# A gated spectral mixer with its gradients on one core: the opening's first folds ordered behind the last scaling of the second token block

## The chip, the core and the metric

The kernel runs on one core of a Trainium2 chip. A core has five engines, each with its own instruction queue that runs strictly in the order in which it was written: TensorE (PE, matrix products, with its weight loads shown as PEld), VectorE (DVE), ScalarE (ACT), GpSimd (POOL) and SyncE (SP). SP here does nothing but issue DMAs; POOL and ACT issue some too. Engines wait for one another through semaphores. The metric is the device time of one execution in microseconds (us); several executions are timed and the median is given. Beside them one execution is recorded by the hardware profiler, and that record is what this document reads.

## The reference, cut to what matters

A forward pass of two branches, mixed by a gate that depends on the token, and then the gradient of everything:

```python
g = sigmoid((x * gate_w).sum(-1, keepdims=True))
a = irfft2(rfft2(x) * (w_r + 1j * w_i))              # spectral branch, over tokens and features
h = relu(x @ w1 + b1); b = (h * h) @ w2 + b2       # dense branch, of the same x
out = g * a + (1 - g) * b
grads = vjp(out)(grad_out)     # for x, w_r, w_i, w1, b1, w2, b2, gate_w
```

There are 2048 tokens of 1024 features, 3584 hidden units, and everything in memory is bf16. The gradient of the dense branch's output is `grad_out` scaled by `1 - g`, one factor per token; that of the spectral branch is `grad_out` scaled by `g`.

## The kernel before

**What the opening does.** Tokens are handled as 16 rows (tiles) of 128 tokens, four rows to a block. For each block four things have to happen before its products can run: the four rows of `x` are loaded into `xsrc` buffers and turned (transposed on TensorE against an identity into a PSUM tile `pt`, then copied to `xT`); the gate of the block is computed; the four rows of `grad_out`, loaded into `dbn`, are scaled in place by `omg` = 1 - g; and the scaled rows are turned the same way into `dbT`. `turn_x`, `turn_grad`, `gate_of` and `gate` do these. `gate_of` (L724) is one long DVE instruction for each row, `x * gate_w` with a running sum; `gate` (L731, L732, L734) is two tiny sigmoids on ACT over the four sums and then four DVE scalings. The two `pt` tiles are used in turn, so that a third transposition waits until the copy of the first is through.

**The products.** Chains of eight matmuls into one PSUM bank. `ph` (L808 in half widths, L821) is a hidden block: x by w1; ACT empties it with a ReLU (L822), and a square (L795) makes `h2T`. `pd` (L828) is the gradient at the hidden layer, `dbT` by the transposed w2; DVE empties it with one instruction (L832, `dhT`). In the opening `ph` and `pd` share two banks, so each chain also waits for the eviction of the one before the last.

**The first stage of the spectral branch.** `first_stage` runs in between, as a generator that the opening's loop advances now and then. It takes pairs of rows (`xs[0]`, `xs[1]`, ..., tiles named `src`, loaded by `ahead_to`, first on SP's queue). `folds` makes sums and differences of a pair on DVE: two into `uv` (L272, L273), then L277, L278, L283 and L284 into `f`, with tiny ACT copies between (L279, L281, L285). `row_stage` then multiplies on TensorE (`pk`, L293) and ACT copies the result to `ft` (L297). `first_columns` follows (`pu`, L325, emptied by three ACT instructions L303 to L307), then two more DVE instructions (L312, L313) and stores.

**What sets the order.** Nobody writes the queues by hand: a scheduler takes the program, its dependencies and priorities and emits each engine's queue. Its freedom is limited with ties. `after(ins, earlier, NoSync)` adds a dependency that orders `ins` behind `earlier` for the scheduler, and without a wait of its own on the chip where both are on the same engine; `after` without that argument also makes `ins` wait. The name `later["last"]` holds the newest eviction of a `pd` product (set in `back_`, L883), and `first_stage` ties its steps to it: the first two folds of each pair, the first matmul of `row_stage` and of `first_columns`, and, through `ahead_to`, the loads of the next pair. The first stage begins in the loop over blocks at k = 0, right behind the gate of the second block:

```python
if k + 1 < NT // 4:
    gate(4 * (k + 1))
if k + 2 < NT // 4:
    rows_of_x(k + 2)
if k == 0:
    ahead_to(1)
    stage = first_stage()
next(stage)
```

At that point the newest `pd` eviction is the second one of the first block (the one before the two that follow in the loop). `next(stage)` runs `folds` for pair 0, the first `row_stage`, and `ahead_to(2)`, which loads pair 2.

Of the kernel before, what the change touches and what calls it, by code (L numbers as in the profile page):

```python
# [14 lines left out]
ALU = mybir.AluOpType  # L15
# [126 lines left out]
def kernel(  # L142
# [22 lines left out]
    nc = tc.nc  # L165
# [43 lines left out]
    gcol, omg, gpg, dgs, dsc = (cols(n, [NT]) for n in ("gcol", "omg", "gpg", "dgs", "dsc"))  # L209
# [40 lines left out]
    def after(ins, earlier, wait=mybir.DependencyClass.Sync):  # L250

        if earlier is not None:
            info = mybir.DependencyInfo(wait, mybir.DependencyReason.DATA)
            tc.add_manual_dep(ins.ins, earlier.ins.name, info, reason="paced")
# [15 lines left out]
    def folds(fb, xt, earlier=None):  # L270
        uv = fb.tile([P, 2, 2, H], FDT, name="uv", tag="uv")
        after(V(out=uv[:, :, 0, :], in0=xt[:, :, 0:H], in1=xt[:, :, H:D], op=ALU.add), earlier, mybir.DependencyClass.NoSync)  # L272
        after(V(out=uv[:, :, 1, :], in0=xt[:, :, 0:H], in1=xt[:, :, H:D], op=ALU.subtract), earlier, mybir.DependencyClass.NoSync)  # L273

        f = fb.tile([P, 2, 6, Q + 2], FDT, name="f", tag="f", bufs=2)
        a0, a1 = uv[:, :, :, 1:Q], uv[:, :, :, H - 1 : Q : -1]
        V(out=f[:, :, 0:2, 1:Q], in0=a0, in1=a1, op=ALU.add)  # L277
        V(out=f[:, :, 2:4, 1:Q], in0=a0, in1=a1, op=ALU.subtract)  # L278
        nc.scalar.copy(out=f[:, :, 3:0:-2, 0], in_=uv[:, :, 1, 0 : Q + 1 : Q])  # L279

        nc.scalar.copy(out=f[:, :, 0:3:2, 0 : Q + 1 : Q], in_=uv[:, :, 0:1, 0 : Q + 1 : Q].to_broadcast([P, 2, 2, 2]))  # L281
        b0, b1 = f[:, :, 0:3:2, 0:P], f[:, :, 0:3:2, Q:P:-1]
        V(out=f[:, :, 4:6, 0:P], in0=b0, in1=b1, op=ALU.add)  # L283
        V(out=f[:, :, 4:6, P:Q], in0=b0, in1=b1, op=ALU.subtract)  # L284
        nc.scalar.copy(out=f[:, :, 5, P::-P], in_=f[:, :, 0:3:2, P])  # L285
        return f

    def row_stage(fb, f, kmat, earlier=None):
        pk = fps.tile([P, 8, P], FP32, name="pk", tag="ps2", bufs=2)
        even = [(row, slice(o, o + P)) for row, o in ((5, P), (4, 0), (4, P), (5, 0))]  # L290
        odd = [(row, slice(o, Q, 2)) for row, o in ((3, 0), (3, 1), (1, 1), (1, 0))]
        for b, (row, o) in enumerate(even + odd):
            first_ = mm(pk[:, b, :], lhsT=f[:, row, o], rhs=kmat[:, b // 6, :], start=True, stop=True)  # L293
            if b == 0:
                after(first_, earlier, mybir.DependencyClass.NoSync)
        ft = fb.tile([P, 8, P], FDT, name="ft", tag="ft", bufs=2)
        nc.scalar.copy(out=ft[:], in_=pk[:])  # L297
        return ft

    def first_columns(cf, t, ft, u, w, earlier=None):  # L300
        pu = fps.tile([P, 2, H], FP32, name="pu", tag="ps2", bufs=2)
        column_stage(pu, ft, cf, earlier)
        nc.scalar.copy(out=w[:, t].rearrange("p c x g i -> p (c x g i)"), in_=pu[:, 1, :])  # L303
        uv = u[:, t].rearrange("p (c h g i) -> p c h g i", c=2, h=2, g=4)
        even = pu[:, 0, :].rearrange("p (g c h i) -> p c h g i", g=2, c=2, h=2)
        nc.scalar.copy(out=uv[:, 0, :, 0::2, :], in_=even[:, 0])
        nc.scalar.mul(out=uv[:, 1, :, 0::2, :], in_=even[:, 1], mul=flip[:])  # L307

    def odd_columns(T, i, u, w):
        uv = u[:].rearrange("p t (c h g i) -> p (t c) h g i", c=2, h=2, g=4)  # L310
        X, Y = (w[:].rearrange("p t c x g i -> p (t c) x g i")[:, :, x] for x in range(2))
        V(out=uv[:, :, 0, 1::2, :], in0=X, in1=Y, op=ALU.add)  # L312
        V(out=uv[:, :, 1, 3::-2, ::-1], in0=X, in1=Y, op=ALU.subtract)  # L313
        nc.gpsimd.tensor_copy(out=edge[:, :, T, i : i + 2], in_=u[:, :, 0::H].rearrange("p t x -> p x t"))
        moved(z_scr, T, i, u, True)
# [377 lines left out]
    dbn = db_p.tile([P, NT, D], BF16, name="dbn", tag="dbn")  # L693
# [4 lines left out]
    later = {}  # L698
# [28 lines left out]
    def gate(i0):  # L727

        c_ = slice(i0, i0 + 4)
        pg = pgs[:, c_]  # L730
        nc.scalar.activation(omg[:, c_], pg, ACT.Sigmoid, scale=-1.0)  # L731
        nc.scalar.activation(gcol[:, c_], pg, ACT.Sigmoid)  # L732
        for i in range(i0, i0 + 4):
            nc.vector.tensor_scalar(out=dbn[:, i, :], in0=dbn[:, i, :], scalar1=omg[:, i : i + 1], scalar2=None, op0=ALU.mult)  # L734

    def ahead_to(n, earlier=None):
        for j in range(len(xs), min(n + 1, NT)):
            xs[j] = f1.tile([P, 2, D], BF16, name="src", tag="src", bufs=3)
            for t in range(2):
                T, i = divmod(2 * j + t, NT)  # L740
                after((ld if j < 3 else st)(out=xs[j][:, t, :], in_=(go_perm if T else x_perm)[i]), earlier)

    def first_stage():
        f, kg = {0: folds(f1, xs[0], later["last"])}, {}
        for j in range(NT):
            T, i = divmod(2 * j, NT)
            ft = {}
            for t in range(2):
                ft[t] = row_stage(f1, f[j][:, t], kg.pop(2 * j + t)[:] if T else kf[:], later["last"])
                if t == 0:  # L750
                    ahead_to(j + 2, later["last"])
                yield
                if t == 0 and j + 1 < NT:
                    for n in range(2 * j + 2, 2 * j + 4) if 2 * j + 2 >= NT else ():
                        kg[n] = f1.tile([P, 2, P], FDT, name="kg", tag="kg", bufs=3)
                        g_ = gcol[:, n - NT : n - NT + 1]
                        scaled = nc.vector.tensor_scalar(out=kg[n][:], in0=kf[:], scalar1=g_, scalar2=None, op0=ALU.mult)
                        after(scaled, later["last"], mybir.DependencyClass.NoSync)
                    f[j + 1] = folds(f1, xs[j + 1], later["last"])
            u = f1.tile([P, 2, D], FDT, name="u", tag="xsrc", bufs=3)  # L760
            w = f1.tile([P, 2, 2, 2, 2, P // 2], FDT, name="w", tag="w")
            for t in range(2):
                first_columns(cf, t, ft[t], u, w, later["last"])
                if t:
                    odd_columns(T, i, u, w)
                yield
        f1_s.close()
# [1051 lines left out]
    def rows_of_grad(k, n=4, lo=0):  # L1819
        for i in range(4 * k + lo, 4 * k + lo + n):  # L1820
            ld(out=dbn[:, i, :], in_=go_perm[i])
# [7 lines left out]
    def turn_grad(i):  # L1829
        turn_tile(dbT, i, dbn[:, i, :], nc.scalar.copy if i in (1, 3) else nc.vector.tensor_copy)  # L1830
# [36 lines left out]
    for k in range(NT // 4):  # L1867
        i = 4 * k
        if k + 1 < NT // 4:
            rows_of_grad(k + 1)  # L1870
        next(units)
        if k:
            turn_grad(i), turn_grad(i + 1)
        next(units)
        turn_grad(i + 2) if k else gate(0)
        next(units)
        if k:
            turn_grad(i + 3)
        else:
            for to, name in ((kf, "kf"), (flip, "flip"), (sel, "sel"), (cf, "cf")):  # L1880
                after(st(out=to[:], in_=cten[name].ap()), later["newest"])
            for n in range(4):
                turn_grad(n)
        next(units)
        if stage:
            next(stage)
        next(units)
        if k + 1 < NT // 4:
            turn_x(i + 4), turn_x(i + 5)
        next(units)  # L1890
        if k + 1 < NT // 4:
            turn_x(i + 6), turn_x(i + 7)
        next(units)
        for n in ((), (0,), (4, 8), (12,))[k]:
            after(st(out=db_scr[:, n : n + 4, :], in_=dbn[:, n : n + 4, :]), later["last"])
        if k + 1 < NT // 4:
            gate(4 * (k + 1))
        if k + 2 < NT // 4:
            rows_of_x(k + 2)
        if k == 0:  # L1900
            ahead_to(1)
            stage = first_stage()
        next(stage)
        if k == 3:
            for _ in later["x_sums"](0):
                pass
        next(units)
        next(stage)
# [45 lines left out]
    out = later["out"]  # L1954
# [36 lines left out]
```

## Time and profile before

| what | value |
|---|---|
| median of 3 executions | 1196.62 us (1193.79, 1196.62, 1200.95) |
| the profiled execution | 1195.43 us |
| its span, first to last instruction | 1193.6 us |
| mean granted clock of TensorE | 0.999 of full |
| PE busy | 1174.1 us |
| DVE, ACT, POOL busy | 895.3, 531.0, 388.6 us |

The profiled execution's own time is 1.83 us longer than its span. A line of a timeline gives the start in us from the beginning of the span, the duration (for several merged instructions: of the group), the engine, the line of the kernel, the operation, the tile written and the tiles read, the shape, and how many instructions were merged; in brackets stands how long the engine had been idle before and what ended that. Matmuls overlap, so the duration of one group reaches a little past the start of the next; the step from group to group is the time that counts. A few matmul records are missing from a trace, so that a chain of eight may show as seven.

### The profile page before, as it was taken

To read this page: it belongs to the slowest core of one execution; us is meant where nothing else is said; L and a number is where in the kernel's file an instruction comes from. 1 tells how busy PE (TensorE), PEld (TensorE's weight loads), DVE (VectorE), ACT (ScalarE), POOL (GpSimd) and SP (SyncE) were. 2 spreads that over 40 slices of the span, in tenths; PEclk is the share of its full clock that TensorE was granted. 3 is DMA by queue.
4 is the path that set the end of the run, shared out by engine and by line. 5 is a ranking of instruction groups with operands and counts; after the bars stand their busy time and mean duration, and the time that the engine had idled before them with its cause. 6 is when DMAs were issued, how large, how long until landed. Compare 5 with 4: busy or idle time off the path is not lost.

```text
span 1193.6 us, 19422 instructions
## 1 busy us (share of the span) xinstructions
PE 1174.1 (98%) x7198; PEld 643.2 (54%) x7291; DVE 895.3 (75%) x1598; ACT 531.0 (44%) x961; POOL 388.6 (33%) x618
## 2 busy tenths in 40 slices
PE   8899999999999999999999999999999999999998
PEld 6555555444444444444446999998544444444444
DVE  5888887688989787877537666666786677976757
ACT  5577888577777773445224565654200010000000
POOL 0224443565857683764231332221001100000000
PEclk9999999999999999999999999999999999999999
DMA  9898585676969879889996999995889999564530
GB/s 255 279 261 245 176 210 178 204 202 176 241 175 214 254 249 179 208 177 228 205 225 139 236 231 246 249 210 158 259 194 235 247 283 282 178 195 149 180 125 36
DMA packets 329464, 249.84 MB, mean 209 GB/s; under 512 B 187912, under 2 KB 287658, under 8 KB 328858
## 3 DMA queue, kind: packets, MB, share of 16 engines
q1 hardware_dynamic: 268352, 112.12, 44.7%
q0 software_dynamic: 35136, 111.72, 29.6%
q10 hardware_dynamic: 25882, 24.76, 7.2%
q8 instruction: 57, 0.93, 0.3%
q14 instruction: 37, 0.30, 0.1%
HBM read 114.82 MB, written 89.67 MB: 171 GB/s over the span
## 4 chain that ended last, share of the span: by engine, by line
PE 72%; DVE 15%; issue 4%; DMA 3%; ACT 3%; POOL 1%; SPq 1%; ACTq 0%; another core or an unknown queue 0%; DVEq 0%; POOLq 0%
PE pX L1277 15%; PE xX L1578 14%; PE pV L1277 11%; PE pd L828 8%; PE xV L1578 7%; PE ph L929 4%; PE xZ L1578 3%; PE ph L821 2%; DVE rT L948 2%; DVE dhT L832 1%; PE pui L325 1%; DVE tt L453 1%; PE pki L635 1%; PE pu L325 1%; PE pk L293 1%
## 5 line engine op out<-in xcount | busy, mean ns | idle before, releaser
L828 PE MATMUL pd<-dbT,w2T 128*128 128x512 bf16 x862 | 207.9, 380 | 3.7 <-DVE dhT L832 1.6
L828 PEld LDWEIGHTS <-w2T 128*128 128x128 bf16 x896 | 86.7, 98 | 106.0 <-issue 7.4
L1578 PEld LDWEIGHTS <-dS 128*128 128x128 f16 x686 | 66.4, 98 | 78.6 <-issue 3.0
L832 DVE SCALAR_TENSOR_TENSOR dhT<-pd,rT 128x512 bf16<-128x512 f32 x112 | 76.5, 683 | 33.4 <-PE pd L828 33.0
L1629 POOL DMA_DIRECT2D out_dram<-ot x32 | 17.4, 544 | 245.8 <-DVE ot L1685 128.0
L1695 ACT ACTIVATE w2br<-w2br,dsc 128x512 f32<-128x512 bf16 x8 | 5.8, 724 | 173.8 <-DVE ot L1685 117.4
L1578 PE MATMUL xX<-oT,dS 128*128 128x512 f16 x336 | 76.4, 379 | 0.2 <-DVE eR L1607 0.2
L1293 ACT COPY u<-pX 128x512 f32<-128x512 f32 x56 | 32.8, 586 | 90.5 <-PE pX L1277 84.9
L1578 PEld LDWEIGHTS <-odd 128*128 128x128 bf16 (+1 forms) x462 | 44.8, 98 | 51.5 <-issue 0.9
L1578 PEld LDWEIGHTS <-even 128*128 128x128 bf16 (+1 forms) x448 | 43.7, 98 | 52.6 <-issue 0.7
L1277 PEld LDWEIGHTS <-T 128*128 128x128 f16 x672 | 64.6, 98 | 7.4 <-issue 0.2
L949 ACT ACTIVATE rT<-rT 128x512 bf16<-128x512 bf16 x69 | 43.4, 629 | 44.2 <-DVE rT L948 43.7
L795 ACT ACTIVATE h2T<-rT 128x1024 bf16<-128x1024 bf16 x56 | 59.7, 1065 | 0.2
L1297 DVE TENSOR_TENSOR whi<-pV,u 128x512 bf16<-128x512 f32 x28 | 19.3, 688 | 47.2 <-ACT u L1293 47.1
L1277 PEld LDWEIGHTS <-S 128*128 128x128 f16 x336 | 32.5, 98 | 40.8 <-DVE S L1209 1.9
L491 POOL DMA_DIRECT2D y_scr<-pc x64 | 47.2, 738 | 18.6 <-DVE pc L488 11.3
L453 DVE TENSOR_TENSOR tt<-x,w 128x1028 f16<-128x1028 f16 (+1 forms) x64 | 43.9, 719 | 10.6 <-ACT x L445 4.6
L1277 PEld LDWEIGHTS <-resL 128*128 128x128 bf16 x448 | 43.1, 98 | 4.9
L1277 PEld LDWEIGHTS <-resR 128*128 128x128 f16 (+1 forms) x448 | 43.0, 98 | 4.9 <-issue 0.2
L860 POOL DMA_DIRECT2D h2T_scr<-h2T x28 | 20.9, 746 | 70.1 <-ACT h2T L795 43.3
L1297 DVE TENSOR_TENSOR wlo<-pV,u 128x512 bf16<-128x512 f32 x28 | 19.2, 687 | 32.0 <-PE pV L1277 31.9
L239 POOL DMA_DIRECT2D r<-y_scr x48 | 28.0, 588 | 41.7 <-ACT re L614 33.1
(382 smaller groups left out, 2797.9 us busy)
## 6 DMA issues: line engine op xcount, KB each, us to landing
h2T_scr<-h2T POOLq DMA_DIRECT2D x28, 512.0 KB, 4.4
dhT_scr<-dhT POOLq DMA_DIRECT2D x28, 512.0 KB, 5.3
y_scr<-pc POOLq DMA_DIRECT2D x64, 128.0 KB, 4.2
ax_scr<-yo POOLq DMA_DIRECT2D x16, 512.0 KB, 5.5
out_dram<-ot POOLq DMA_DIRECT2D x31, 256.0 KB, 3.9
z<-z_scr ACTq DMA_DIRECT2D x60, 128.0 KB, 3.8
out_dram<-whi POOLq DMA_DIRECT2D x28, 256.0 KB, 4.9
out_dram<-wlo POOLq DMA_DIRECT2D x28, 256.0 KB, 5.6
```

What stands on the lines that cost most here:

```text
L239: st(out=a, in_=b) if stored else st(out=b, in_=a)
L453: V(out=tt[:, k, :, :, 0:W], in0=x[:, a : a + 2, :, 0:W], in1=by, op=ALU.mult)
L491: st(out=columns_of(y_scr, c, h), in_=pc[:, n])
L795: after(nc.scalar.activation(h2T, rT, ACT.Square), behind_, mybir.DependencyClass.NoSync)
L828: turn["PE"] = mm(pd[:], lhsT=w_[:, ec, fc % FGC * P : (fc % FGC + 1) * P], rhs=dbT[:, ec, ss], start=(ec == 0), stop=(ec == DC - 1),)
L832: return STT(out=dhT, in0=pd[:], scalar=2.0, in1=rT, op0=ALU.mult, op1=ALU.mult, accum_out=gb1part[:, fc, sb : sb + 1],)
L929: turn["PE"] = mm(acc[:], lhsT=lhs[:, t, :], rhs=rhs[:, t, :], start=start and t == 0, stop=t == KH - 1, skip_group_check=True,)
L949: nc.scalar.activation(rT, rT, ACT.Relu)
L1277: self.mm = mm(out, lhsT=lhs[:, t, m * P : (m + 1) * P], rhs=rhs[:, t, :], start=start and t + a == 0, stop=t == KH - 1, skip_group_check= ...
L1293: turn["ACT"] = nc.scalar.copy(out=t_[:], in_=self.X[:])
L1297: turn["DVE"] = self.added = V(out=self.half(row, j), in0=self.sums(acc), in1=self.sums(t_), op=ALU.add)
L1578: ins = mm(acc, lhsT=lhs[:, fc, :], rhs=rhs[:, fc, :], start=start and fc == 0, stop=fc == KH - 1 and bias is None, skip_group_check=True,)
```

## The change

The last of the four scalings is handed out of `gate`, and the loop puts the one of the second block (rows 4 to 7, `gate(4)` at k = 0) into `later["last"]` just before it starts the first stage. The next `pd` eviction overwrites that again, as before.

```diff
@@ in gate
         for i in range(i0, i0 + 4):
-            nc.vector.tensor_scalar(out=dbn[:, i, :], in0=dbn[:, i, :], scalar1=omg[:, i : i + 1], scalar2=None, op0=ALU.mult)
+            scaled = nc.vector.tensor_scalar(out=dbn[:, i, :], in0=dbn[:, i, :], scalar1=omg[:, i : i + 1], scalar2=None, op0=ALU.mult)
+        return scaled
@@ in the loop over blocks
         if k + 1 < NT // 4:
-            gate(4 * (k + 1))
+            scaled = gate(4 * (k + 1))
         if k + 2 < NT // 4:
             rows_of_x(k + 2)
         if k == 0:
             ahead_to(1)
+            later["last"] = scaled
             stage = first_stage()
         next(stage)
```

So pair 0's two folds, the first `row_stage` and the loads of pair 2 are tied to that scaling. No instruction is added or removed. The queues around the place, before and after:

| queue | before | after |
|---|---|---|
| DVE | sums of rows 4, 5; dhT; sum of row 6; L272; sum of row 7; L273; 4 scalings; L277, L278; dhT; L283, L284; folds of pair 1; dbT copy; ... | sums of rows 4, 5; dhT; sums of rows 6, 7; 4 scalings; L272, L273; dhT; L277, L278; dbT copy; L283, L284; folds of pair 1; dbT copy; ... |
| ACT | ReLU; two sigmoids; ReLU; L279; square; ... | sigmoid; ReLU; sigmoid; ReLU; square; L279; ... |
| PE | pd; turn rows 4, 5; pd but one matmul; 16 pk; last of pd; 2 of ph; turn row 6; rest of ph; turn row 7; ... | pd; turn rows 4, 5; pd; turn row 6; 2 of ph; 16 pk; rest of ph; turn row 7; ... |
| SP | pair 1's second row; pair 2; 8 rows of grad_out; ... | pair 1's second row; 3 rows of grad_out; pair 2; 5 rows of grad_out; ... |
| POOL | | the same |

Some 20 us on, a few transposes, `pd` matmuls and the next block's folds stand one or two places apart from before; from about 60 us the queues are the same.

## The prediction

> **What bounds the kernel now.** I read the page first, then the granted clock in slices of one microsecond, then the timelines of PE, DVE, ACT and SP between 20 and 45 us. From the page, the shares of the engines:
>
> ```profile
> PE 1174.1 (98%) x7198; PEld 643.2 (54%) x7291; DVE 895.3 (75%) x1598; ACT 531.0 (44%) x961; POOL 388.6 (33%) x618
> ```
>
> PE is busy for 1174.1 of 1193.6 us, so all its idle time is 19.5 us, and an edit that adds and removes no work has little to win. The stretch from 30 us on holds its largest hole. By microseconds (window, length, PE busy and matmuls, granted clock, DMA share, GB/s):
>
> ```profile
> 30.00:31.00 1.00, 0.31 (x2) 1.00 1.06 391
> ...
> 33.00:34.00 1.00, 0.00 (x0) 0.86 1.06 385
> 34.00:35.00 1.00, 0.84 (x9) 0.50 1.04 383
> ...
> 36.00:37.00 1.00, 1.00 (x4) 0.50 1.06 393
> 37.00:38.00 1.00, 1.00 (x5) 0.94 1.06 391
> ```
>
> PE stops at 30.31, its clock falls to one half at about 33.86 (0.86 of that slice) and returns at about 37.06. The timeline of PE (start, length, line, operation, how many, idle before and what ended it):
>
> ```profile
> 24.83 3.69 PE L808 MATMUL ph<-xT,w1g 128*128 128x256 bf16 x32
> 28.42 1.89 PE L828 MATMUL pd<-dbT,w2T 128*128 128x512 bf16 x7
> 34.16 1.89 PE L709 MATMUL pt<-identb,dbn 128*128 128x128 bf16 x16 [3.85 <-DVE dbn L734]
> 35.84 2.32 PE L828 MATMUL pd<-dbT,w2T 128*128 128x512 bf16 x7
> 38.08 1.07 PE L293 MATMUL pk<-kf,f 128*128 128x128 f16 x16
> ...
> 39.20 0.59 PE L821 MATMUL ph<-xT,w1g 128*128 128x512 bf16 x2
> 39.64 0.61 PE L709 MATMUL pt<-identb,dbn 128*128 128x128 bf16 x8
> ...
> 42.31 1.89 PE L821 MATMUL ph<-xT,w1g 128*128 128x512 bf16 x8
> 44.04 0.40 PE L325 MATMUL pu<-cf,ft 128*128 128x128 f16 x4
> 44.27 1.89 PE L828 MATMUL pd<-dbT,w2T 128*128 128x512 bf16 x8
> ```
>
> The transposes of grad_out rows 4 and 5 wait 3.85 us for their scaling (L734). DVE tells why it is late:
>
> ```profile
> 25.60 1.22 DVE L724 SCALAR_TENSOR_TENSOR Sw<-xsrc,Sw 128x1024 bf16<-128x1024 bf16 x1
> ...
> 31.26 0.69 DVE L272 TENSOR_TENSOR uv<-src 128x1024 f16<-128x1024 bf16 x1 [4.43 <-DMA src<-in_A_x_dram]
> 31.87 1.22 DVE L724 SCALAR_TENSOR_TENSOR Sw<-xsrc,Sw 128x1024 bf16<-128x1024 bf16 x1
> 33.02 0.08 DVE L724 DVE_READ_ACCUMULATOR Sw<-xsrc,Sw 128x1 f32 x1
> 33.02 0.68 DVE L273 TENSOR_TENSOR uv<-src 128x1024 f16<-128x1024 bf16 x1
> 33.62 1.67 DVE L734 TENSOR_SCALAR dbn<-dbn,omg 128x1024 bf16<-128x1024 bf16 x4
> 35.20 0.68 DVE L277 TENSOR_TENSOR f<-uv 128x1020 f16<-128x1020 f16 x1
> ...
> 36.41 0.68 DVE L832 SCALAR_TENSOR_TENSOR dhT<-pd,rT 128x512 bf16<-128x512 f32 x1
> ...
> 37.36 0.42 DVE L284 TENSOR_TENSOR f<-f 128x512 f16<-128x512 f16 x1
> ```
>
> The first fold (L272) stands ahead of the fourth gate sum and idles DVE for 4.43 us until its source has landed; the sum, the gate and the scalings queue behind it. That load releases PE here.
>
> **The change, part by part.** It adds and removes no instruction. Compared engine by engine, the streams differ from about 27 to 60 us only and are the same afterwards; POOL's is the same throughout.
>
> *Fold behind scaling: the hole.* DVE's order becomes fourth sum, four scalings, then both folds. The sum starts at 26.83 (the third one's start and 1.23 us to its read-out, as from 31.87 to 33.10) and is read out at 28.1. What the gate needs of ACT and of the loads of grad_out:
>
> ```profile
> 27.68 0.69 ACT L822 ACTIVATE rT<-ph,b1col 128x512 bf16<-128x512 f32 x1 [1.18 <-PE ph L808]
> 33.13 0.21 ACT L731 ACTIVATE omg<-pgs 128x4 f32<-128x4 f32 x1 [4.76 <-DVE Sw L724]
> 33.24 0.19 ACT L732 ACTIVATE gcol<-pgs 128x4 f32<-128x4 f32 x1
> L1821 SPq DMA_DIRECT2D dbn<-in_grad_out_dram x1: 430/430/430, 21.9 to 21.9; - x1
> DMA to landing us min/median/max: 6.5/6.5/6.5
> ```
>
> The sigmoid takes 0.21 us and ends by 28.4; row 7, the last of the four, lands at 21.94 + 6.5 = 28.4. The scalings run from 28.4 to 30.1, and row 4 is ready near 28.9, before PE is through with its pd product at 30.3. The hole goes (3.85 us), and with it the half clock: 37.06 - 34.16 = 2.9 us of PE work at half speed, of which half, 1.45 us, was lost. Removed: 3.85 + 1.45 = **5.30 us**. Were the 28.4 of row 7 late, only its own transposes, two products later, would wait.
>
> *ACT: the sigmoid passes a ReLU.* In the new order the sigmoid stands ahead of the ReLU of 27.68, which empties the bank that the pd product of 28.42 takes (it started 0.05 us after that ReLU's end). The ReLU now starts after the sigmoid, at about 28.24 (ACT goes on 0.11 us after a tiny instruction: 33.13 to 33.24), ends at 28.93, and pd starts at about 28.97: **0.55 us** lost. Bounds: nothing if the sum comes out 0.5 us sooner, 0.7 (one ReLU) if it comes later; I take 0.55.
>
> *DVE: the wait for the source takes in other work.* The source load was issued before any moved instruction, so I keep the fold at 31.26. Behind it now stand, in this order, the second fold, the eviction dhT of the pd product, L277, L278 and the first copy dbT of transposed rows (L710). At DVE's spacing (0.60 us per full-width instruction: 33.02 to 33.62) the copy runs from 31.26 + 5 x 0.60 = 34.3 to 34.96. PE meanwhile: pd 28.97 to 30.70, transposes of rows 4 and 5 to 31.59 (0.89, the step of 16 at full clock: 38.08 to 38.98 for pk), the second pd to 33.32 (1.73 for a chain of eight: 42.31 to 44.04). Next is the transpose of row 6, which reuses the bank that this copy empties: it starts at 35.02. A new wait of **1.70 us**, in place of the pk matmuls, which stood there and covered it. Bounds: 0 if the copy were free in time, 3.85 if it took as long as the old hole; I take 1.70, from the rows.
>
> *First stage later.* pk waits for L284 and the tiny ACT copy after it. L284 follows the dbT copy, at 35.22, ends 35.64, the ACT copy (0.21) at 35.9; PE has meanwhile done row 6's transposes (0.44) and two ph matmuls (0.43) and is at 35.9 as well: nothing. Then pk to 36.83, the rest of ph to 38.12, row 7's transposes to 38.57, four pu to 38.97. The next ph takes the bank of the ph before, whose ReLU stands on ACT behind both ft copies, of which this is the first:
>
> ```profile
> 38.73 1.01 ACT L297 CAST ft<-pk 128x1024 f16<-128x1024 f32 x1 [0.71 <-PE pk L293]
> ```
>
> From pk's first half at 36.5 the two run to 38.43 (0.9 us a step and a tiny copy between), the ReLU to 39.12, and ph starts at 39.17: **0.20 us**. It ends at 40.90, pu's rest takes 0.23, and the next pd can start near 41.2 (its bank's eviction follows two folds and ends at 39.25). In the profile that pd starts at 44.27.
>
> *SP and POOL.* Two loads of the third source pair now wait for the last scaling, with five rows of grad_out, one of w1 and four of x queued behind on SP:
>
> ```profile
> 28.48 1.68 SPq L741 DMA_DIRECT2D src<-in_A_x_dram  x3
> 30.50 5.66 SPq L1821 DMA_DIRECT2D dbn<-in_grad_out_dram  x8
> 35.39 0.73 POOL L860 DMA_DIRECT2D h2T_scr<-h2T  x1 [16.98 <-ACT h2T L795]
> ...
> L741 SPq DMA_DIRECT2D src<-in_A_x_dram x1: 328/328/328, 28.5 to 28.5; - x1
> DMA to landing us min/median/max: 6.0/6.0/6.0
> 52.87 1.67 DVE L734 TENSOR_SCALAR dbn<-dbn,omg 128x1024 bf16<-128x1024 bf16 x4
> ```
>
> SP reaches that wait after one src and three dbn issues, four steps of 0.68 us, at 31.2, when the scaling has been over for 1.1 us: nothing. Those grad_out rows are next needed at the scaling of 52.87; without that cover a late SP would cost its delay. POOL's store of h2T comes with its squares about 3.4 us sooner, into loads that already run at 1.0 of the DMA engines: 0.5 MB at 385 GB/s is 1.4 us for the source row issued at 28.48, which lands at 34.5 by its 6.0 us, and is needed at 35.56: 0 to 0.4 us, covered by the 0.7 us that row 7's transposes leave.
>
> *Sum.* 5.30 - 0.55 - 1.70 - 0.20 = 2.85 us; the walked timeline gives 44.27 - 41.2 = 3.07. I take **3.0 us**. From there on the order is the old one, PE has 98% and shifts as a block. The profiled execution took 1195.43 us (span 1193.6 and 1.83 around it), 1.2 below the median of 1196.62: 1195.43 - 3.0 = 1192.4 for its like, **1193.6** against the median.
>
> **Rivals.**
>
> (a) *The new waits are smaller.* Only ACT's 0.55 us remains: 4.75 us won, 1191.9. For it: a source that lands 1.7 us sooner would do. Against: its landing is in the trace, and nothing ahead of it moves. 0.12.
>
> (b) *The new wait trips the clock again.* Then 1.45 us go back: 1.55 won, 1195.1. For it: the gap of 1.70 us lies between 0.79, which left the clock at 1.00, and 3.85, in which it fell 3.55 us after PE had stopped. Against: it is nearer to the first.
>
> ```profile
> 11.67 1.92 PE L808 MATMUL ph<-xT,w1g 128*128 128x256 bf16 x16 [0.79 <-DVE xT L710]
> ...
> 11.00:12.00 1.00, 0.33 (x3) 1.00 1.79 320
> ```
>
> Chance 0.13. The Trainium skill, "TensorE: Matmul & The Clock Gate", Part 4, says that transposes do not count as PE activity in the same way; the quiet time before the gate would then be 1.70 + 0.44 = 2.14 us, and the sum by that rule could be this rival's. The 16 transposes at 34.16 ran at half clock; whether they counted this trace does not say.
>
> (c) *Given back later.* DVE fills the stretches behind and PE just waits elsewhere: 1196.6. For it:
>
> ```profile
> 70.00:80.00 10.00, 9.95 (x82) 6.07 (x82) 9.98 (x21) 5.76 (x15) 3.82 (x7) 1.00 0.83 271
> ```
>
> (PE, PEld, DVE, ACT, POOL busy). DVE has 9.98 of 10 us there. Against: PE has 9.95, and DVE's work hangs on PE's products, so both move together; no load is tied to absolute time. 0.12.
>
> (d) *Slower: the second source pair.* The folds of xs[1] now head DVE with a dbT copy behind them. If its last row lands d later than 34.5, row 7's transposes wait d - 1.75 us. From d = 4.75 the change loses. With d = 6.5 the wait is 4.75, the clock falls again (1.45), and 3.2 us are lost: 1199.8; a further us for each beyond. Against: it takes 10.8 us from issue where the load now takes 6.0, and the moved traffic explains 1.4. 0.07.
>
> (e) *It doesn't do what it says*: the tie is no wait, only order, and another release holds the scalings (row 7's landing). Each us by which they were later than 30.3 at row 4 costs one; at 3 us it is 1196.6 again. 0.04.
>
> **How the numbers follow.** The forecast has 0.52. Single times of the unchanged kernel run from 1193.79 to 1200.95, so the bound of 0.5% (6 us) is about what a measurement tells from no change. Only (a) with a favourable median reaches 1190.6: faster 0.09. (d) and an unfavourable median: slower 0.07; same 0.84. The range takes in (a), (b) and (c) with 1.5 us of scatter of a median: 1190.4 to 1198.1. The likeliest case's own is 1191.5 to 1195.5.
>
> **What would show it.** Right: no idle PE before the transposes of rows 4 and 5, clock 1.00 through 30 to 40 us, scaling at 28.4, a fold at 31.3 idling DVE for some 1.2 us behind the scalings, a PE wait near 33.3 on a dbT copy of about 1.7, and the pd of 44.27 near 41.2. Wrong: a clock of 0.50 after 35, a source row landing past 35.6, or a pd near 41.2 with the end unmoved.

## The result, and the profile after

| kernel | executions | median, us | lowest to highest | ratio to before, 95% interval |
|---|---|---|---|---|
| before | 22 | 1193.82 | 1191.89 to 1200.95 | |
| changed | 22 | 1191.18 | 1189.94 to 1208.15 | 0.9976 (0.9964 to 0.9987) |

The medians are 2.64 us apart. The ratio, here and below, leaves out slow executions, those over 1.5% above the fastest of their kernel (here 1208.15 alone); by it the change wins 0.24%, with an interval of 0.13% to 0.36%: clear of no change, and less than the 0.5% that the prediction counts as a difference. The forecast was 3.0 us won. Its level of 1193.6 lies 2.4 us too high, since it started from a median of three executions, 1196.62, and 22 of them give 1193.82.

The profiled execution of the changed kernel took 1194.43 us (span 1192.7), more than 18 of its 22, so its timeline shows one of the less lucky ones. The page's shares, for the whole span:

```profile
PE 1176.9 (99%) x7291; PEld 641.4 (54%) x7291; DVE 895.7 (75%) x1598; ACT 530.7 (44%) x961; POOL 388.3 (33%) x618
```

PE stands at 99% where 98% stood before. The difference comes partly from records: this trace has all 7291 matmuls, the one of before 7198. The timeline of PE in the opening (start, length, line, operation, count, idle before and what ended it):

```profile
24.80 3.69 PE L809 MATMUL ph<-xT,w1g 128*128 128x256 bf16 x32
28.94 1.89 PE L829 MATMUL pd<-dbT,w2T 128*128 128x512 bf16 x8 [0.45 <-ACT rT L823]
30.66 1.06 PE L709 MATMUL pt<-identb,dbn 128*128 128x128 bf16 x16
31.56 1.89 PE L829 MATMUL pd<-dbT,w2T 128*128 128x512 bf16 x8
37.05 0.61 PE L709 MATMUL pt<-identb,dbn 128*128 128x128 bf16 x8 [3.60 <-DVE dbT L710]
37.49 0.59 PE L822 MATMUL ph<-xT,w1g 128*128 128x512 bf16 x2
37.97 1.07 PE L293 MATMUL pk<-kf,f 128*128 128x128 f16 x16
...
41.29 1.89 PE L822 MATMUL ph<-xT,w1g 128*128 128x512 bf16 x8 [0.23 <-ACT rT L823]
...
43.30 1.89 PE L829 MATMUL pd<-dbT,w2T 128*128 128x512 bf16 x8
```

The transposes of rows 4 and 5 (30.66) follow their product at once: the old hole is gone. A new wait of 3.60 us stands before row 6's transposes, almost as long as the 3.85 us that went. DVE, in the same columns, says why:

```profile
28.54 1.08 DVE L734 TENSOR_SCALAR dbn<-dbn,omg 128x1024 bf16<-128x1024 bf16 x2 [0.47 <-DMA dbn<-in_grad_out_dram]
...
30.50 0.49 DVE L734 TENSOR_SCALAR dbn<-dbn,omg 128x1024 bf16<-128x1024 bf16 x1 [0.19 <-DMA dbn<-in_grad_out_dram]
33.29 0.69 DVE L272 TENSOR_TENSOR uv<-src 128x1024 f16<-128x1024 bf16 x1 [2.30 <-DMA src<-in_A_x_dram]
...
36.31 0.68 DVE L710 COPY dbT<-pt 128x1024 bf16<-128x1024 bf16 x1
```

In this execution the first source pair landed at 33.29 us, in the one of before at 31.26 (here and below the landing is read from the start of the fold that waits for it, 0.1 us after the last piece). The copy of the transposed rows stands behind that fold, and PE waits for the copy.

A measure for what follows is the stretch from the start of the half-width `ph` product to the start of the next pair's first `pd` product. Before it is 24.83 to 44.27, 19.44 us; after, 24.80 to 43.30, 18.50. The 0.94 us between them is all that the two spans differ by (1193.6 and 1192.7). So these two executions, in which the source landed 2.03 us later after the change than before it, show less than the medians do; where the other 1.7 us are, this pair can't show.

### The profile page after: what moved, and what is told of

Its sections match the earlier page's. It is cut to its first block, busy times and chain, and to the rows that moved or that the text cites. A ratio compares the mean times of both kernels' runs of the same rounds, so it can differ in the third digit from the quotient of the medians.

```text
span 1192.7 us, 19514 instructions
## 1 busy us (share of the span) xinstructions
PE 1176.9 (99%) x7291; PEld 641.4 (54%) x7291; DVE 895.7 (75%) x1598; ACT 530.7 (44%) x961; POOL 388.3 (33%) x618
## 4 chain that ended last, share of the span: by engine, by line
PE 74%; DVE 15%; ACT 4%; DMA 3%; issue 3%; ACTq 0%; POOL 0%; SPq 0%; DVEq 0%
PE pX L1278 15%; PE xX L1579 14%; PE pV L1278 12%; PE pd L829 9%; PE xV L1579 7%; PE ph L930 5%; PE xZ L1579 3%; PE ph L822 2%; DVE rT L949 2%; DVE dhT L833 2%; PE pui L325 1%; DVE tt L453 1%; PE pki L635 1%; PE pu L325 1%; DMA w2T<-in_B_w_dram 1%
```

## The experiments

### Both kernels once more

The kernels as they are.

> The kernel before, recorded once more. Theory A: the hole before the transposes of rows 4 and 5 is as long as pair 0's second row is late (landing plus 2.9 us minus 30.3), and the clock falls if the hole passes about 3.4 us. Rival: a hole of 3.85 us and half clock whatever the landing.

> The changed kernel, recorded once more, to see how far its opening differs between executions. Theory A (the fold now takes DVE's head and waits there for pair 0's second row, so the new PE wait follows that row's landing): the PE wait before row 6's transposes is the landing of the row plus 3.7 us minus 33.3, so 1.7 us if the row lands at 31.3 and 3.6 if at 33.3; whatever the landing, no PE idle before the transposes of rows 4 and 5. Rival B (the PE wait is a fixed price of the new DVE order): about 3.6 us again, with the fold starting early. Clock: 1.00 through the opening for a wait under 3.4 us. Median 1190 to 1193, 0.2 to 0.3% under the kernel before.

The kernel before took 1194.72 us in one execution; the changed one 1191.03 (median of 12), ratio 0.9972 (0.9956 to 0.9987). PE in the new execution of the kernel before:

```profile
27.76 1.89 PE L828 MATMUL pd<-dbT,w2T 128*128 128x512 bf16 x8
32.34 1.89 PE L709 MATMUL pt<-identb,dbn 128*128 128x128 bf16 x16 [2.70 <-DVE dbn L734]
```

Its source landed at 29.45 and its hole was 2.70 us (expected from that landing: 2.05, but PE came to the hole 0.66 us sooner than in the first execution). Its clock, in slices of one microsecond, still fell, against the 3.4 us that were expected as the bound:

```profile
32.00:33.00 1.00, 0.66 (x7) 0.66 (x8) 1.00 (x4) 1.00 (x3) 0.00 (x0) 0.56 1.01 371
...
35.00:36.00 1.00, 1.00 (x5) 0.38 (x4) 1.00 (x5) 0.00 (x1) 0.00 (x0) 0.73 1.05 387
```

A slice at 0.56 has 0.88 us at half clock, one at 0.73 has 0.54: half clock from 32.12 to 35.54. From 32.34 on PE worked in it, so half of 3.20, 1.60 us, was lost. And PE in the new execution of the changed kernel:

```profile
28.50 1.89 PE L829 MATMUL pd<-dbT,w2T 128*128 128x512 bf16 x8 [0.45 <-ACT rT L823]
...
33.25 0.61 PE L709 MATMUL pt<-identb,dbn 128*128 128x128 bf16 x8 [0.25 <-DVE dbT L710]
...
37.49 1.89 PE L822 MATMUL ph<-xT,w1g 128*128 128x512 bf16 x8 [0.23 <-ACT rT L823]
```

Here the source was in time, so the rival, a wait of 3.6 us whatever the landing, is out: the new wait is 0.25 us, and the whole stretch has 0.93 us of waits. The stretches are 18.31 us (before) and 15.15 (after), 3.16 apart. By terms: 2.70 and 1.60 removed, 0.45, 0.25 and 0.23 added, 3.37.

### The source loaded sooner, in both

One edit to either kernel: on SP the first source pair's loads go ahead of the third block's first x rows. (`src_early` is the changed kernel with it, `before_src_early` the kernel before.)

```diff
+        if k == 0:
+            ahead_to(0)
         if k + 2 < NT // 4:
             rows_of_x(k + 2)
```

> The changed kernel with pair 0's two loads issued ahead of block 2's first two rows of x; nothing else moves on any queue. So pair 0's second row is issued early and a row of x, which is needed much later, takes its place on SP behind the second turned load of w2. Theory A: the fold starts when the scalings end (30.1 to 31.0) and the PE wait before row 6's transposes shrinks to 0.5 to 1.5 us; 1 to 2 us faster than the changed kernel. Rival B: PE waits 3.6 us as in the profile of the changed kernel, same time. Rival C (the landing is set by the throughput of the DMA engines, which are full there, not by SP): the row lands less than 1 us earlier and the time is the same.

> The kernel before with pair 0's two loads issued ahead of block 2's first two rows of x; the old tie and the old order of DVE are kept. Theory A (the old order costs only what the source is late): the first fold waits to about 29.8 instead of 31.3, the scalings start about 32.1, the PE hole shrinks from 3.85 to about 2.3 us and the clock does not fall: 2.5 to 3 us faster than before, about level with the changed kernel. Rival B (it is the order that costs, not the landing): the hole stays near 3.8 us, same time as before.

The changed kernel: 1191.2 us, ratio 0.9968 (0.9954 to 0.9982), stretch 15.15, waits 0.45, 0.25 and 0.23 as above. The 1 to 2 us expected did not come: the profiled execution without the edit had its source in time as well. The kernel before: 1192.66 us, ratio 0.9981 (0.9969 to 0.9994). PE in that one:

```profile
30.63 1.07 PE L709 MATMUL pt<-identb,dbn 128*128 128x128 bf16 x16 [0.68 <-DVE dbn L734]
...
34.55 1.07 PE L293 MATMUL pk<-kf,f 128*128 128x128 f16 x16 [1.35 <-ACT f L285]
```

With the source at 27.73 the old order leaves a hole of 0.68 us, the clock stays at 1.00 throughout, and 1.35 us come back as a wait of pk; the stretch is 16.29. Expected were a hole of 2.3 us and a time level with the changed kernel's; the hole came out shorter, the time 1.6 us above. So moving two loads does half to two thirds of what the change does (1.9 of 3.5 us by the medians, 0.19% of 0.28% by the ratios, whose intervals overlap), and it adds nothing to the changed kernel that can be measured: what both attack is the same thing, a fold that idles DVE ahead of work that PE needs. The four stretches (15.15, 15.15, 16.29, 18.31) are 0, 0, 1.14 and 3.16 above the shortest, the four times, measured together (changed, again 1191.03; source sooner; before with the source sooner; before, again, one execution) 0, 0.2, 1.6 and 3.7 above the lowest.

### The folds alone

Only the folds of the first pair take the new tie; the loads of the third pair and the first stage's matmuls keep the old one.

```diff
-    def first_stage():
-        f, kg = {0: folds(f1, xs[0], later["last"])}, {}
+    def first_stage(behind_):
+        f, kg = {0: folds(f1, xs[0], behind_)}, {}
...
-            later["last"] = scaled
-            stage = first_stage()
+            stage = first_stage(scaled)
```

> Only the first source pair's folds are tied behind the last scaling; the loads of the third source pair and the first stage's matmuls keep their tie behind the newest product. Theory (what the change wins it wins on VectorE alone, and the move on SP and POOL is worth nothing): the same as the changed kernel, 1191.0 us, within 0.3, with the first dbT tile copied before TensorE needs it. Rival (the earlier start of the third pair's load is part of the gain): 0.5 to 1.0 us slower than the changed kernel, with a fold of the third pair waiting for its source.

1191.86 us, ratio 0.998 (0.997 to 0.999): 0.9 us above the 1191.0 expected and 0.6 beyond its bound, though the intervals of the two kernels overlap. The rival's sign, a fold of the third pair waiting for its source, isn't there: from 24 to 120 us DVE waits for a source once, 0.9 us, ahead of the first fold. PE pays for that one, where the theory had the copy in time:

```profile
34.40 0.61 PE L709 MATMUL pt<-identb,dbn 128*128 128x128 bf16 x8 [1.24 <-DVE dbT L710]
```

The moved loads of the third pair show no effect of their own; by the times alone up to 1.0 us for them stays open (1191.86 against the changed kernel's medians of 1190.9 to 1191.18).

### The changed kernel a third time

> The changed kernel once more, beside the version with the three edits. Theory (its time hangs on when the first pair's second source row lands): 1191 us, some 3 us below the kernel before, its executions 1190 to 1198, and in the profile the wait before the third row's transposes is 0.25 us plus what VectorE idles for the source ahead of the first fold, less about 0.1 us. Rival (the spread has nothing to do with that row): the wait and the idle time don't go together.

1190.9 us, two of 12 executions above the expected 1198 (highest 1201.39); ratio 0.9979 (0.9954 to 1.0005), an interval that takes in no change. Its profiled execution, DVE first:

```profile
30.44 0.69 DVE L272 TENSOR_TENSOR uv<-src 128x1024 f16<-128x1024 bf16 x1 [1.34 <-DMA src<-in_A_x_dram]
```

and PE:

```profile
34.20 0.61 PE L709 MATMUL pt<-identb,dbn 128*128 128x128 bf16 x8 [1.67 <-DVE dbT L710]
```

The theory adds 1.34 of idle DVE to 0.25, takes off 0.1 and has 1.49; 1.67 was measured. So the two go together, within 0.2 us. In the first execution of the changed kernel the same sum gives 2.45 for 3.60 us, since there the scalings, too, had waited, 0.86 us for rows of grad_out. What holds throughout is the distance from the first fold:

| execution | first fold starts | row 6's transposes start | difference | PE's wait |
|---|---|---|---|---|
| changed | 33.29 | 37.05 | 3.76 | 3.60 |
| changed, again | 29.49 | 33.25 | 3.76 | 0.25 |
| changed, third | 30.44 | 34.20 | 3.76 | 1.67 |
| source sooner | 30.09 | 33.84 | 3.75 | 0.25 |
| folds alone | 30.63 | 34.40 | 3.77 | 1.24 |

When the source lands decides the rest. On SP the second row of the first pair is issued behind a wait for a transposing load of w2; SP's waits from 20 to 40 us, of the changed kernel, its second and its third execution (line, what it waited for, us in total, times, longest):

```profile
SPq L742 <- DMA w2T<-in_B_w_dram: 4.8, 1, 4.8
```

```profile
SPq L742 <- DMA w2T<-in_B_w_dram: 0.5, 1, 0.5
```

```profile
SPq L742 <- DMA w2T<-in_B_w_dram: 2.1, 1, 2.1
```

4.8, 0.5 and 2.1 us go with folds at 33.29, 29.49 and 30.44. The traces settle the chain. The w2 load counts its completion on semaphore 102, and the source row's issue waits for that semaphore and then uses it itself. The last count of the w2 load comes at 27.99, 23.71 and 25.13 us, the row is issued at 28.01, 23.73 and 25.14, and its last piece lands 5.2 us later each time, at 33.19, 28.93 and 30.34. (At 28.93 the scalings were still running; there the fold waited for them alone.) What varies is the w2 load, which took 11.0, 7.3 and 9.4 us from issue to landing. The new wait is 3.35 us longer in the first execution than in the second, nearly all of the 3.50 us between their times (1194.43 and 1190.93). In the third it is 1.42 us longer, of 3.22 us; another 0.9 us there are a wait of ph for a `dhT` behind a late store, so this row isn't the only cause of scatter.

### The folds behind the copies

The first stage starts one block later in the program, once rows 4 and 5 have been turned, and is tied behind the copy of the second of them; its first products and the loads of the third pair move with it. DVE: four scalings, `dhT`, two copies, then the folds. (Cut: `turn_grad` hands out its copy.)

```diff
         if k:
-            turn_grad(i), turn_grad(i + 1)
+            turn_grad(i)
+            copied = turn_grad(i + 1)
+        if k == 1:
+            later["last"] = copied
+            stage = first_stage()
+            next(stage)
...
+        if k == 1:
+            next(stage)
...
         if k == 0:
             ahead_to(1)
-            later["last"] = scaled
-            stage = first_stage()
-        next(stage)
+        if k:
+            next(stage)
...
-        next(stage)
+        if k:
+            next(stage)
```

> The changed kernel, with the folds behind the copies of the second token block's first two turned rows instead of ahead of them. Theory (folds ahead of the copies are what makes TensorE wait there, 0.25 us where the source is in time and 3.60 us where it is late): the wait before the third row's transposes goes, the stretch shrinks from 15.15 to about 14.9, the time is 0.2 to 0.3 us below the changed kernel's, and a late source row no longer shows in it. Rival (the folds are then late for the first stage's own matmuls, and the wait moves there): pk or pu waits 0.5 to 1.5 us for f or ft, and the time is 0.3 to 1.3 us above the changed kernel's.

1190.79 us, ratio 0.9969 (0.9955 to 0.9982). PE:

```profile
29.84 1.89 PE L829 MATMUL pd<-dbT,w2T 128*128 128x512 bf16 x7 [0.45 <-ACT rT L823]
...
34.19 0.61 PE L709 MATMUL pt<-identb,dbn 128*128 128x128 bf16 x8
...
38.26 1.07 PE L293 MATMUL pk<-kf,f 128*128 128x128 f16 x16 [0.21 <-ACT f L285]
```

No wait is left before row 6's transposes, and of the rival's wait for `f` 0.21 us came instead of 0.5 to 1.5. The stretch is 14.82 us, 0.33 below the changed kernel's best; the time is 0.1 to 0.4 us below the changed kernel's three medians, which is within their scatter. This execution's source was in time, so that the order also stands up to a late one follows from the queues and isn't shown by it.

### The ReLU ahead of the sigmoids

The changed kernel, with both sigmoids of the second block's gate tied behind the ReLU that one of them passes; alone, and then with the source sooner. (Cut: `later["relus"]` collects the ReLUs of the hidden blocks.)

```diff
-        nc.scalar.activation(omg[:, c_], pg, ACT.Sigmoid, scale=-1.0)
-        nc.scalar.activation(gcol[:, c_], pg, ACT.Sigmoid)
+        gated = nc.scalar.activation(omg[:, c_], pg, ACT.Sigmoid, scale=-1.0)
+        gated2 = nc.scalar.activation(gcol[:, c_], pg, ACT.Sigmoid)
+        if i0 == 4:
+            after(gated, later["relus"][4], mybir.DependencyClass.NoSync)
+            after(gated2, later["relus"][4], mybir.DependencyClass.NoSync)
```

> The changed kernel, with the two sigmoids of the second token block's gate tied behind the ReLU that they passed. Theory (the 0.45 us that the first product of the pair waits for rT is all on the path): that wait goes, the stretch from the half-width product to the pair's next product shrinks from 15.15 to about 14.7 us, and the time is 0.45 us below the changed kernel's, 1190.6. Rival (the sigmoid then comes some 0.6 us later, the scalings and the folds behind it too, and the wait before the third row's transposes grows by as much): that wait grows from 0.25 to 0.7 or more, and the time is the changed kernel's, 1191.0, or up to 0.3 more.

1193.22 us, from 1190.44 to 1235.54, ratio 0.9983 (0.9963 to 1.0004): too wide to judge. The profiled execution took 1198.23 us and met a late source, at 34.57. PE in it:

```profile
28.66 1.90 PE L832 MATMUL pd<-dbT,w2T 128*128 128x512 bf16 x7
...
36.52 1.31 PE L825 MATMUL ph<-xT,w1g 128*128 128x512 bf16 x3 [3.35 <-DVE dhT L836]
38.33 1.01 PE L709 MATMUL pt<-identb,dbn 128*128 128x128 bf16 x8 [0.49 <-DVE dbT L710]
```

The 0.45 us wait before pd is gone, as meant. The edit also let three ph matmuls go ahead of row 6's transposes, and the late source then took 3.35 us of PE and the clock with it (slices of one microsecond):

```profile
36.00:37.00 1.00, 0.48 (x2) 0.24 (x2) 1.00 (x4) 0.10 (x1) 0.00 (x0) 0.84 1.06 410
37.00:38.00 1.00, 0.84 (x2) 0.15 (x1) 1.00 (x3) 0.23 (x1) 0.00 (x0) 0.50 1.04 399
...
40.00:41.00 1.00, 1.00 (x17) 1.00 (x17) 1.00 (x3) 0.31 (x1) 0.00 (x0) 0.95 1.04 381
```

With the source out of the way:

> The sigmoids behind the ReLU again, now with the first source pair's loads ahead on SP, so that the source is in time and the folds stand ahead of the copies as in the changed kernel. Theory (the ReLU's 0.45 us is won in full): stretch 14.7 us, time 0.4 us below the changed kernel's. Rival (the scalings start some 0.6 us later, the first fold with them, and the third row's transposes follow the first fold by 3.76 us): the 0.45 us wait goes and the 0.25 us wait grows to 0.6 to 0.8, stretch 15.1 us, time that of the changed kernel.

1191.41 us, ratio 0.9974 (0.9964 to 0.9984), no better than the changed kernel. PE:

```profile
33.11 0.61 PE L709 MATMUL pt<-identb,dbn 128*128 128x128 bf16 x8 [0.27 <-DVE dbT L710]
...
37.35 1.89 PE L825 MATMUL ph<-xT,w1g 128*128 128x512 bf16 x8 [0.58 <-ACT rT L826]
```

The 0.45 us went, the wait before the later ph grew from 0.23 to 0.58, and 0.85 us of waits stand against 0.93. The stretch is 15.26 us, not 14.7; four more transposes of the next block stand inside it (0.22 us), so for the same work it would be 15.04. The rival was right that it is given back, and named the wrong place: the wait for the copy hardly grew, since three ph matmuls had come ahead of it on PE. PE, with less ph left to do, then met the ReLU behind the ft copies earlier. Row 6's transposes follow the first fold by 3.76 and 3.75 us in these two versions as well.

### Both edits, and all three

Folds behind the copies with the ReLU ahead (`copies_relu`), and the source sooner as well (`copies_relu_early`).

> Both edits together: folds behind the two copies, sigmoids behind the ReLU. Theory: no wait of 0.2 us or more is left on TensorE in this stretch, 14.4 to 14.5 us long, and the time is 0.7 us below the changed kernel's, 1190.3. Rival (with the scaling and then the folds later, the first stage's matmuls are the next to wait): the gain of the one edit is given back by the other, and the time is 1191.0 or more.

> Folds behind the two copies, sigmoids behind the ReLU, and the first source pair's loads ahead of the third block's first x rows on SP. Theory (in the stretch only TensorE's waits count, and a source row in time gives nothing more once the folds stand behind the copies): the stretch is 14.3 us as with the two edits, the time 0.6 to 0.8 us below the changed kernel's of the same call, and its runs lie closer together. Rival (the third block's x rows, now two issues later, are late for its transposes or its sums): the time is the changed kernel's or up to 1 us more, with a wait for xsrc ahead of the third block's transposes.

1190.57 us, ratio 0.9964 (0.9951 to 0.9978), and 1190.77 us, ratio 0.9962 (0.9944 to 0.9981). Stretches 14.26 and 14.27 us. The one wait that is left in the stretch of the second, from its timeline of PE:

```profile
36.50 1.07 PE L293 MATMUL pk<-kf,f 128*128 128x128 f16 x16 [0.21 <-ACT f L285]
```

The stretches came out as expected, 0.9 us below 15.15; the times didn't follow. They lie 0.1 to 0.6 us below the changed kernel's three medians (1191.18, 1191.03, 1190.9), with overlapping intervals: beside the kernel before these are the lowest ratios found, but a gain over the changed kernel isn't shown. What does differ is the upper end. Of the 45 executions of the changed kernel that the ratios count, 8 took over 1194 us; of the 48 of the five changed versions with the source sooner or the folds behind the copies, 1 did. (Of the two other versions with the changed kernel's weak spot, the one with the ReLU ahead had 2 in 10 and the one with the folds alone none in 12, so this is a sign and no proof.)

## Why the prediction was right, point by point

**The hole goes.** Right, in all three profiled executions: rows 4 and 5 are turned without a wait, and the clock stays at 1.00 through the stretch. *Removed 5.30 us* was right for the execution that it was read from and is no constant: 2.70 + 1.60 = 4.30 in the next one. A source that lands 1.81 us sooner made the hole 1.15 shorter, PE having come to it 0.66 us sooner as well. The clock's part of it is not there in a typical execution. A fall of 3.4 us takes 0.0014 off the mean granted clock, and of the 88 executions of the kernel before that were timed beside the experiments and that the ratios count, 45 show 1.000. These have a median of 1193.58; 38 of the changed kernel's 45 show 1.000 and have 1190.93. So 2.65 us are won with no clock lost on either side. The prediction read the 0.86 of a slice as the moment of the fall. Read as a share (0.28 us at half clock), the half clock ran from 33.72 to 37.12, and the lost part is 1.48 instead of 1.45.

**ACT, 0.55 us.** Measured 0.45, in each profiled execution whose sigmoid passes the ReLU. The undoing of it showed that this term was on the path and yet not to be had alone: 0.35 us came back at the next ReLU.

**The new wait, 1.70 us.** The mechanism is exact: the prediction put row 6's transposes 3.76 us after the first fold (31.26 and 35.02), and the five executions show 3.75 to 3.77. The size was not one: 0.25, 1.67 and 3.60 us in three executions of one kernel. What failed is the step "I keep the fold at 31.26". The landing is not a property of the program, and against (a) the prediction said "its landing is in the trace, and nothing ahead of it moves", taking one draw for a constant.

**First stage later, 0.20 us.** Measured 0.23, on the ReLU behind the ft copies as described.

**Why 3.0 still came out near 2.64.** The two terms with the wrong certainty share their cause: an early source shrinks the hole and the new wait together. With an early source in both (folds at 29.45 and 29.49) the sum is 4.30 - 0.93 = 3.37, the stretch says 3.16, and the medians of 22 executions 2.64. Without the clock's 1.60 the same sum would be 1.77; with the first hole's 3.85 it would be 2.92. How long the hole is in a typical execution no run shows. The walked timeline had the next pair's pd near 41.2; it came at 43.30, 39.51 and 40.46. That the forecast hit the difference is partly luck: it comes from this cancelling rather than from knowing either term, and it counted 1.45 us of clock that about half the executions never lost.

**SP and POOL, nothing.** No later wait for the moved loads was seen, so the cost is small; the landing of the source varied with what SP had issued long before, not with what the change moved.

**The rivals.** (a), smaller waits, is what the changed kernel does when the source is in time: waits of 0.93 us. Its price of 4.75 us did not come, since the hole had been smaller too. (b) did not happen in the changed kernel's profiles, not even at 3.60 us, but in the version with the ReLU ahead a late source cost the clock at 3.35; the last section shows what the 3.60 us escaped by. (c) did not happen to the change: what the stretch won in the first pair of profiles (0.94 us) is what the span won (0.9). Whether it happened to the small edits after it stays open: from the next pair's pd to the end of the span they take 1150.0 to 1151.4 us, the changed kernel 1149.4, 1149.6 and 1151.9. (d) was not seen, no fold of the second pair waits. (e) is out: in the first execution the scalings did wait for rows of grad_out, 0.86 us, but were through before PE needed them.

## What to carry to other kernels

Before an instruction is moved ahead of or behind a load's consumer, look at several executions for when that load lands: a profile gives one draw, and a term that hangs on it is a range. An in-order engine should not meet an uncertain wait ahead of work that the bound engine needs soon; moving the wait behind one such piece of work only hands it on to the next, and putting it behind all of them is the order that should stand up to a late load. Terms that hang on the same landing move together, so their difference is known better than each. A lost clock that one profile shows need not be there in most executions.

## What the runs showed of the hardware

- **Whether the clock fell followed from how busy PE was in fixed steps of 3.41 us, and not from the length of the idle time alone.** It fell after idle times of 3.85 us (before), 2.70 (before, again) and 3.35 (the ReLU ahead), and did not after 3.60 (changed). Counted from PE's stop it came 3.41, 2.48 and 3.50 us later, in the last case 0.16 us after PE had started again. Once fallen it stayed for the same time: 33.72 to 37.12, 32.12 to 35.54, 36.68 to 40.10, or 3.40, 3.42 and 3.42 us. The clock records of the traces say more. In each of the 13 profiled executions every change of the clock lies a whole number of steps of 3.413 us behind the first record of full clock (3.89 to 7.08 us into the span); the three falls lie 8, 8 and 9 steps behind it. In the step that ended with the fall PE was busy for 0.01, 0.93 and 0.16 us. In the changed kernel's execution an edge at 35.25 cuts the 3.60 us in two, and the two steps have 1.61 and 1.62 us of busy PE. Over the whole spans of all 13, each step with at most 1.17 us of busy PE ended with a fall (seven steps, four of them at the end of the program), and no step with 1.61 us or more did. So the bound lies between 1.17 and 1.61 us of 3.41, and for idle times near that length it is chance where the edges fall. The Trainium skill, "TensorE: Matmul & The Clock Gate", Part 1, has a free-running window of about 3.4 us that doesn't start with the work; the steps and the varying delay agree with that. The 0.93 us speak against the need of a whole idle window: they were ordinary matmuls, and the first transposes came 0.22 us after that fall, so whether transposes count as activity does not enter there.
- **A DMA issue on SP can wait for the completion of another transfer that it has no data in common with.** The second source row waited 0.5 to 4.8 us for the transposing load of w2, with which it shares a completion semaphore (number 102 in the traces). The difference between executions of one program in that wait is larger than what the change wins.
